# Cosine router after a state-space scan: work moved between VectorE, ScalarE and GpSimd, first steps reordered, three shared PSUM banks for the experts' turned tiles

## The chip, the cores and the metric

The program runs on one core of one Trainium2 chip. The metric is the device time in microseconds of one execution. Five engines run their own queues in order and meet at semaphores: TensorE (PE; its weight loads are listed apart as PEld), VectorE (DVE), ScalarE (ACT), GpSimd (POOL) and SyncE (SP, which here only issues DMAs).

## The reference

A Mamba-2 scan over 4 batches, 8 heads and 768 positions (head width 32, state width 16) gives 3072 tokens of 256 numbers. Each token then goes to one of 8 experts, the one whose embedding has the largest cosine with it, and its two-layer result is scaled by the softmax of that choice.

```python
for c in range(nc):                       # chunks of the sequence, state carried on
    cum = np.cumsum(la, axis=-1)          # la = log(clip(a))
    L = np.exp(cum[..., :, None] - cum[..., None, :]) * causal
    y_intra = np.einsum('bhij,bhjd->bhid', np.einsum('bhin,bhjn->bhij', Cc, Bc) * L, xc)
    y_inter = np.einsum('bhin,bhnd->bhid', Cc, state) * np.exp(cum)[..., None]
...
logits = xn @ en.T / tau                  # xn, en: rows over their norm + 1e-6
expert_idx = np.argmax(logits, axis=1)
h = np.maximum(x[mask] @ w1[e], 0.0)      # for every expert e
out[mask] = gate_w[mask, None] * (h @ w2[e])
```

## The kernel before

The scan cuts the sequence into 6 chunks of 128 positions. Decays are made as running products (`decays`) and put on the operands: C times the decay up to its position (`scale_c`, tile `cp`) and x times the inverse (`scale_x`, tile `xs`), so that the product C B^T needs only a causal mask. B is written twice with half of its state rows set to zero (`split_b`, tile `bz`). A pair p is two of a chunk's four batches, so there are 12 pairs, two for each chunk.

The order is written out by hand. `begin_scan` holds the first steps; `mamba` then runs steps s = 1 to 11. In step s TensorE makes the scores of pair s (`scores`, L467, into `pgA` and `pgB`), the outputs of pair s-1 (L499, L508, into `py`), in odd steps the sums for the next state (L526, into `pz`), the tokens of pair s-2 (`tokens`, L557, which also gives their logits), and the routing's matmuls: ranks (L353) in even steps, a table (L411) in odd ones. `masks` (L473 to 486) clears the acausal half of the scores: `pgA` by a multiplication on VectorE (L478), `pgB` by a copy on ScalarE (L477) and a selection in place on GpSimd (L484). ScalarE then copies the outputs (`yT`, L518) and the tokens (`yt`, L567). VectorE makes the next state from `pz` in odd steps (`states`: V at L542, T at L547, V only after ScalarE's `yt`), then the one-hot choice of expert (`pick`, L329 to L338, called the routing here; the ranks need it). In even steps it makes the places (`places`, L369 to L401, called the placing), and ScalarE a part of them (`hv`, L404). In ScalarE's queue `hv` stands ahead of the next step's mask copy.

SyncE loads a chunk's inputs two chunks ahead and the first expert's weights in parts, and stores the tokens' rows. GpSimd gathers rows for the experts by indirect DMA (`gather`, L708), takes a square root in `squares` (L723), and scatters the results (L796).

The experts (`moe`) run as jobs: two short ones for tokens known early and left over from them (256 and 160 rows), then eight of up to 416 rows in four blocks. A job turns its rows (`turn_x`, L750, two halves, each copied by VectorE at L752), goes up (8 blocks of L760, three PSUM banks in a ring), down (L775), and out (`out`, L789, four blocks turned back, scaled by ScalarE or VectorE, scattered). A ring hands out its banks in turn; a bank is written again only when its last reader is done. `turn_x` has a ring of one bank (3), `out` of two (6 and 7). `gates` makes the softmax factor; its exponential (L737) stands in ScalarE's queue among the `hT` copies.

Of the kernel before, what the change touches and what calls it, by code (L numbers as in the profile page):

```python
# [296 lines left out]

def norm_embeddings(k):
    nc = k.nc
    tau = k.en_tau  # L300
# [4 lines left out]
    nc.gpsimd.tensor_scalar(out=r[:], in0=r[:], scalar1=1e-6, scalar2=None, op0=ALU.add)
    nc.gpsimd.tensor_tensor(out=r[:], in0=r[:], in1=tau[:], op=ALU.mult)
    k.emb_r = r
    k.turn = k.mc.tile([128, 2, Y1], F32, name="turn")
    nc.gpsimd.tensor_copy(out=k.turn[:, 0, 0:128], in_=k.ident[:])
    blocks = lambda v: v.rearrange("p (a s d) -> p a s d", a=2, s=2)  # L310
    for i in range(2):
        nc.gpsimd.tensor_copy(out=blocks(k.turn[:, 1, E:])[:, :, i, :], in_=blocks(k.ident[:])[:, :, 1 - i, :])
# [160 lines left out]
def masks(k, p):  # L473
    nc = k.nc
    s = k.un[p] = Net()
    s.g = k.work.tile([128, 4, 4, Q], F32, name="g", tag="g")
    k.nc.scalar.copy(out=s.g[:, 2:4].rearrange("p q a i -> p q (a i)"), in_=k.pgB[:])  # L477
    nc.vector.tensor_tensor(  # L478
        out=s.g[:, 0:2].rearrange("p q a i -> p (q a) i"),
        in0=k.pgA[:].rearrange("p q (a i) -> p (q a) i", a=4),  # L480
        in1=bc(k.mask[:], [128, 8, Q], 1), op=ALU.mult,
    )
    g = s.g[:, 2:4].rearrange("p q a i -> p (q a) i")
    nc.gpsimd.affine_select(  # L484
        out=g, in_=g, pattern=[[0, 8], [1, Q]], compare_op=ALU.is_ge, fill=0.0, base=0, channel_multiplier=-1
    )
# [609 lines left out]
```

## Time and profile before

| what | time |
|---|---|
| three runs | 305.37, 308.0, 308.25 us; median 308.0 |
| profiled execution | 307.75 us; its span, from the first to the last instruction, 305.9 us |
| busy share of the span | PE 88%, DVE 37%, ACT 28%, POOL 38% |
| mean granted TensorE clock | 0.953 of full speed |
| scan and routing | from 0 to about 84 us |
| experts | from about 84 us to the end |

A row of the timeline shows what an engine did and, in brackets, how long it had stood before and what ended that. A row may merge several instructions; "x32" is their count. [...] Of a busy time of several engines in one stretch, only the engine whose waits are shortest sets the time there.

### The profile page before, as it was taken

How to read it: one execution, taken by the hardware profiler on the slowest of the kernel's cores; microseconds unless marked ns; L12 is line 12 of the kernel's file. 1: busy time of each engine (PE TensorE's matmuls, PEld its weight loads, DVE VectorE, ACT ScalarE, POOL GpSimd, SP SyncE). 2: the span in 40 equal slices, each digit the busy share in tenths (PEclk: the TensorE clock that was granted, in tenths of full speed). 3: DMA queues.
4: the chain of work that ended last, by engine and by line, in shares of the span. 5: the costliest groups of instructions: out<-in, count | busy, mean ns of one | idle time of the engine just before them, and what ended most of it. 6: DMA issues, size and time to landing. Idle time of an engine off the chain costs nothing.

```text
span 305.9 us, 5554 instructions
## 1 busy us (share of the span) xinstructions
PE 267.7 (88%) x2183; PEld 175.7 (57%) x2183; DVE 114.5 (37%) x352; ACT 84.2 (28%) x214; POOL 117.4 (38%) x142
## 2 busy tenths in 40 slices
PE   7388895897989699998999999999999999999980
PEld 6276784785868586554555555555555555555540
DVE  7048778369462342312321330422323042133110
ACT  2136574373323213121203212120330221122010
POOL 3955745464402626206503710740460172015004
PEclk9758999797899999999999999999999999999996
DMA  6801567263497155124340712424060020001001
GB/s 195 333 3 44 200 219 272 75 206 111 110 350 259 48 174 186 42 117 132 109 137 1 224 47 108 141 99 137 20 224 2 0 74 30 0 0 56 0 0 61
DMA packets 20781, 34.78 MB, mean 114 GB/s; under 512 B 2328, under 2 KB 13796, under 8 KB 20752
## 3 DMA queue, kind: packets, MB, share of 16 engines
q1 hardware_dynamic: 17712, 27.94, 27.2%
q0 software_dynamic: 2816, 6.40, 6.9%
q8 instruction: 18, 0.29, 0.4%
q14 instruction: 11, 0.09, 0.1%
q10 hardware_dynamic: 224, 0.06, 0.1%
HBM read 28.26 MB, written 6.65 MB: 114 GB/s over the span
## 4 chain that ended last, share of the span: by engine, by line
PE 50%; issue 26%; DVE 10%; POOL 7%; ACT 3%; DMA 2%; SPq 1%; POOLq 1%; DVEq 0%; ACTq 0%
PE bank L760 17%; PE bank L775 15%; POOL out_dram L796 3%; PE pz L557 3%; PE py L508 3%; PE pgA L467 3%; POOL xg L708 2%; PE py L499 2%; DVE g L478 2%; PE bank L789 2%; DMA in_t<-in_B_dram 1%; PE bank L750 1%; DVE T L547 1%; DVE xT L752 1%; DMA in_c<-in_CT_dram 1%
## 5 line engine op out<-in xcount | busy, mean ns | idle before, releaser
L760 PE MATMUL bank<-xT,w 128*128 128x416 f32 (+2 forms) x288 | 93.9, 477 | 2.0 <-ACT hT L764 1.9
L775 PE MATMUL bank<-hT,w 128*128 128x416 f32 (+2 forms) x288 | 91.7, 476 | 0.0
L760 PEld LDWEIGHTS bank<-xT,w 128*128 128x128 f32 x288 | 52.2, 190 | 36.6 <-issue 32.6
L775 PEld LDWEIGHTS bank<-hT,w 128*128 128x128 f32 x288 | 52.6, 190 | 34.8 <-issue 33.7
L723 POOL TENSOR_TENSOR gr<-gr,half 128x4 f32<-128x4 f32 (+1 forms) x9 | 8.7, 971 | 92.5 <-ACT sq L719 89.1
L796 POOL DMA_INDIRECT out_dram<-yo,to x30 | 29.2, 974 | 36.0 <-ACT yo L795 28.0
L766 DVE TENSOR_SCALAR hT<-bank 128x416 f32<-128x416 f32 (+2 forms) x33 | 18.2, 553 | 60.2 <-PE bank L760 55.8
L708 POOL DMA_INDIRECT xg<-rows,table x30 | 30.5, 1018 | 21.2 <-DVE to_u L440 13.1
L764 ACT ACTIVATE hT<-bank 128x416 f32<-128x416 f32 (+2 forms) x39 | 18.1, 469 | 62.1 <-PE bank L760 56.3
L467 PE MATMUL pgA<-cp,bz 32*128 32x128 f32 x192 | 17.3, 326 | 9.2 <-POOL bz L179 4.3
L734 DVE TENSOR_SCALAR gr<-gr 128x4 f32<-128x4 f32 (+1 forms) x9 | 1.5, 170 | 60.9 <-POOL gr L723 58.2
L484 POOL TENSOR_SCALAR_AFFINE_SELECT g<-g 128x1024 f32<-128x1024 f32 x12 | 13.4, 1114 | 27.4 <-ACT g L477 27.4
L779 ACT COPY yoT<-bank 128x416 f32<-128x416 f32 (+2 forms) x9 | 4.2, 467 | 66.4 <-PE bank L775 66.4
L467 PEld LDWEIGHTS pgA<-cp,bz 32*128 32x128 f32 x192 | 14.8, 227 | 10.5 <-POOL bz L179 4.5
L478 DVE TENSOR_TENSOR g<-pgA,mask 128x1024 f32<-128x1024 f32 x12 | 14.6, 1217 | 10.8 <-PE pgB L467 7.0
L467 PE MATMUL pgB<-cp,bz 32*128 32x128 f32 x192 | 17.4, 328 | 0.0
L750 PE MATMUL bank<-ident,xg 128*128 128x128 f32 x64 | 11.5, 273 | 6.6 <-DVE xT L752 6.6
L508 PE MATMUL py<-g,xs 128*32 128x128 f32 x384 | 15.2, 301 | 2.1 <-issue 2.1
L557 PE MATMUL pz<-turn,yT 128*128 128x136 f32 x96 | 15.9, 312 | 0.1
L477 ACT COPY g<-pgB 128x1024 f32<-128x1024 f32 x12 | 12.1, 1007 | 12.0 <-PE pgB L467 11.3
L750 PEld LDWEIGHTS bank<-ident,xg 128*128 128x128 f32 x64 | 7.8, 139 | 12.7 <-DVE xT L752 7.7
L467 PEld LDWEIGHTS pgB<-cp,bz 32*128 32x128 f32 x192 | 14.6, 225 | 0.0
(195 smaller groups left out, 272.8 us busy)
## 6 DMA issues: line engine op xcount, KB each, us to landing
w<-in_moe_w_dram SPq DMA_DIRECT2D x14, 1024.0 KB, 4.9
rows<-yt SPq DMA_DIRECT2D x12, 264.0 KB, 5.5
in_x<-in_x_dram SPq DMA_DIRECT2D x6, 512.0 KB
w<-in_moe_w_dram SPq DMA_DIRECT2D x8, 256.0 KB, 3.7
in_b<-in_BT_dram SPq DMA_DIRECT2D x6, 256.0 KB, 3.2
in_c<-in_CT_dram SPq DMA_DIRECT2D x6, 256.0 KB
in_t<-in_B_dram SPq DMA_DIRECT2D x6, 256.0 KB
xg<-rows,table POOLq DMA_INDIRECT x30
```

Of the source, the lines that this page charges most:

```text
L467: k.nc.tensor.matmul((k.pgA, k.pgB)[q // 2][:, q % 2, a : a + 128], lhsT=t.bz[r, v, b + i, :], rhs=t.cp[r, b + i, :], start=True, stop=Tru ...
L478: nc.vector.tensor_tensor(out=s.g[:, 0:2].rearrange("p q a i -> p (q a) i"), in0=k.pgA[:].rearrange("p q (a i) -> p (q a) i", a=4), in1=bc ...
L484: nc.gpsimd.affine_select(out=g, in_=g, pattern=[[0, 8], [1, Q]], compare_op=ALU.is_ge, fill=0.0, base=0, channel_multiplier=-1)
L508: nc.tensor.matmul(k.py[g : g + 32, v, 128 * i : 128 * i + 128], lhsT=t.xs[:, b + i, 4 * v + q, :], rhs=s.g[:, q, 2 * i + v, :], start=(c ...
L557: k.nc.tensor.matmul(k.pz[i][:, at : at + Y1], lhsT=yT[:, j, i, :], rhs=k.turn[:, j, :], start=(j == 0), stop=(j == 1), skip_group_check=True,
L708: s.k.nc.gpsimd.indirect_dma_start(out=s.x[0:p, i, 0:TOK], out_offset=None, in_=rows, in_offset=bass.IndirectOffsetOnAxis(ap=s.at[0:p, i : ...
L750: nc.tensor.transpose(t[:, o : o + p], s.x[0:p, i, Y1 * j : Y1 * j + 128], k.ident[:p, :p])
L760: nc.tensor.matmul(t, lhsT=s.w1[:, j, 128 * f : 128 * f + 128], rhs=s.xT[:, j, :], start=(j == 0), stop=(j == KD - 1))
L764: nc.scalar.activation(s.hT[:, f, :], t, ACT.Relu)
L766: nc.vector.tensor_scalar_max(s.hT[:, f, :], t, 0.0)
L775: nc.tensor.matmul(t, lhsT=s.w2[:, f, 128 * j : 128 * j + 128], rhs=s.hT[:, f, :], start=(f == 0), stop=(f == KF - 1))
L796: d = nc.gpsimd.indirect_dma_start(out=k.out[:, :], out_offset=bass.IndirectOffsetOnAxis(ap=s.to[0:p, i : i + 1], axis=0), in_=y[:p], in_o ...
```

## The change

- `split_b` runs on VectorE (for the first two chunks one half stays on ScalarE); before, GpSimd had a half of chunk 0 and both of chunk 1, ScalarE the rest.
- `scale_x` runs on VectorE, one pair in each step (before on GpSimd, two pairs in odd steps). `scale_c` runs on VectorE throughout (before on GpSimd from step 3 on), and stands ahead of `split_b`.
- `masks`: from step 3 on ScalarE copies both `pgB` and `pgA`, and GpSimd selects in both. In steps 0 to 2 `pgA` stays with VectorE.
- First steps: the small copies for `turn` come first on GpSimd and half of the routing's constants later; the embedding's norm is made later, part of it on VectorE; two of the fill matmuls that keep TensorE busy go. `inverse(k, 1)` moves from step 2 to 3, its turn from step 4 to 6.
- Experts: `turn_x` and `out` share one ring of banks 3, 6 and 7. The gathers of the first full job (`begin(1)`) are issued ahead of the first two jobs' squares, and both squares stand together.

```diff
-def split_b(k, c, halves=(0, 1), pool=()):
+def split_b(k, c, act=()):
     t = k.ld[c]
...
+    t.bz = k.work.tile([128, 2, NB, Q], F32, name="bz", tag="bz")
+    for v in range(2):
+        if v in act:
+            k.nc.scalar.activation(t.bz[:, v], t.bt[:], ACT.Copy, scale=k.tmask[:, v : v + 1])
+        else:
+            k.nc.vector.tensor_scalar(
                 out=t.bz[:, v], in0=t.bt[:], scalar1=k.tmask[:, v : v + 1], scalar2=None, op0=ALU.mult
             )
...
-def masks(k, p):
+def masks(k, p, both=True):
...
+    for h in range(2):
+        ps = (k.pgB, k.pgA)[h][:].rearrange("p q (a i) -> p (q a) i", a=4)
+        g = s.g[:, 2 - 2 * h : 4 - 2 * h].rearrange("p q a i -> p (q a) i")
+        if h == 1 and not both:
+            nc.vector.tensor_tensor(out=g, in0=ps, in1=bc(k.mask[:], [128, 8, Q], 1), op=ALU.mult)
+            continue
+        nc.scalar.copy(out=g, in_=ps)
+        nc.gpsimd.affine_select(
+            out=g, in_=g, pattern=[[0, 8], [1, Q]], compare_op=ALU.is_ge, fill=0.0, base=0, channel_multiplier=-1
+        )
...
-    decays(k, 0)
-    norm_embeddings(k)
-    place_consts(k)
-    split_b(k, 0, pool=(1,))
+    first, later, consts = decays(k, 0), decays(k, 1), place_consts(k)
+    turn_consts(k)
+    next(consts)
+    next(first)
+    next(first)
+    split_b(k, 0, act=(0,))
     spread_decays(k, range(4))
     inverse(k, 0)
...
-    fill(k, 2, k.pgA[:, 0, 0:Q])
+    fill(k, 1, k.pgA[:, 0, 0:Q])
     keep_decays(k, 1)
     scores(k, 0)
-    decays(k, 1)
-    scale_x(k, 0, nc.gpsimd)
-    scale_x(k, 1, nc.gpsimd)
-    masks(k, 0)
+    next(later)
+    next(later)
+    norm_embeddings(k)
+    masks(k, 0, both=False)
     scale_c(k, 1, spread_at(k, 0))
+    scale_x(k, 0, nc.vector)
...
-    split_b(k, 1, pool=(0, 1))
+    split_b(k, 1, act=(0,))
...
+    scale_x(k, 1, nc.vector)
+    next(consts)
...
-            masks(k, s)
+            masks(k, s, both=s > 2)
...
-        if s == 4:
+        if s == 6:
             turn_inverse(k, 1, k.py[:, 0, 256:384])
...
+        if s % 2 and c < NC - 1:
+            states(k, c)
+        if s + 2 < NP:
+            scale_c(k, s + 2)
         if s % 2 == 0 and s // 2 + 1 < NC:
             split_b(k, s // 2 + 1)
-        if s % 2 and c < NC - 1:
-            states(k, c)
...
-        if s + 2 < NP:
-            scale_c(k, s + 2, eng=nc.vector if s < 3 else nc.gpsimd)
-        if s % 2 and c + 1 < NC:
-            scale_x(k, 2 * c + 2, nc.gpsimd)
-            scale_x(k, 2 * c + 3, nc.gpsimd)
+        if s + 1 < NP:
+            scale_x(k, s + 1, nc.vector)
...
-        if s == 2:
+        if s == 3:
             inverse(k, 1)
...
-    k.bank = {"hp": ring(banks[0:3]), "xt": ring(banks[3:4]), "yp": ring(banks[4:6]), "ot": ring(banks[6:8])}
+    turned = ring([banks[3], banks[6], banks[7]])
+    k.bank = {"hp": ring(banks[0:3]), "xt": turned, "yp": ring(banks[4:6]), "ot": turned}
...
     load_all_weights(k, 2)
+    begin(1)
     j0.down(0)
     j0.squares()
-    begin(1)
+    jobs[1].squares()
     j0.gates()
     j0.down(1)
     jobs[1].turn_x()
-    jobs[1].squares()
     jobs[1].gates()
```

The first place is VectorE's queue in step 5, from `states` to the start of the routing (L329 before, L332 of the change): before, and then of the change.

```order
L542 TENSOR_TENSOR V<-T,pz_91 128x2x64
L542 TENSOR_TENSOR V<-T,pz_92 128x2x64
L547 TENSOR_TENSOR T<-V,whole 128x256
L420 TENSOR_TENSOR acc<-acc,pz_91 128x64
L329 TENSOR_REDUCE m<-yt 128x4
```

```order
L546 TENSOR_TENSOR V<-T,pz_91 128x2x64
L546 TENSOR_TENSOR V<-T,pz_92 128x2x64
L551 TENSOR_TENSOR T<-V,whole 128x256
L270 TENSOR_TENSOR cp<-in_c,fr 128x256
L423 TENSOR_TENSOR acc<-acc,pz_91 128x64
L279 TENSOR_TENSOR xs<-in_x,rT 128x512
L332 TENSOR_REDUCE m<-yt 128x4
```

A `cp` and an `xs` now stand between the state and the routing.

The second place is VectorE's queue further on, from the routing's last instruction (L338 before, L341 of the change) to the second of the placing: before, and then of the change.

```order
L338 TENSOR_REDUCE ob<-ob 128x8
L478 TENSOR_TENSOR g<-pgA,mask 128x1024
L369 TENSOR_TENSOR oh<-pz_92,ob 128x32
L385 TENSOR_REDUCE row<-oh 128x4
L387 TENSOR_SCALAR hl<-row 128x4
```

```order
L341 TENSOR_REDUCE ob<-ob 128x8
L270 TENSOR_TENSOR cp<-in_c,fr 128x256
L182 TENSOR_SCALAR bz<-in_b,tmask 128x512 x2
L279 TENSOR_TENSOR xs<-in_x,rT 128x512
L372 TENSOR_TENSOR oh<-pz_92,ob 128x32
L388 TENSOR_REDUCE row<-oh 128x4
```

The mask of step 6 is gone from between routing and placing; a `cp`, two halves of `bz` and an `xs` stand there.

The third place is TensorE's queue where one full job's rows are turned, ahead of its `down` (bank names carry their number): before, and then of the change.

```order
L750 MATMUL bank3_1398<-ident_129,xg0_219 128x128 x3
L750 MATMUL bank3_1398<-ident_129,xg0_219 128x32
L750 MATMUL bank3_1398<-ident_129,xg0_219 128x128 x3
L750 MATMUL bank3_1398<-ident_129,xg0_219 128x32
L775 MATMUL bank4_1399<-hT_1677,w2_1_68 128x416 x8
```

```order
L758 MATMUL bank6_1407<-ident_129,xg0_319 128x128 x3
L758 MATMUL bank6_1407<-ident_129,xg0_319 128x32
L758 MATMUL bank7_1408<-ident_129,xg0_319 128x128 x3
L758 MATMUL bank7_1408<-ident_129,xg0_319 128x32
L783 MATMUL bank4_1405<-hT_1683,w2_1_68 128x416 x8
```

The two halves now lie in two banks; the order of the instructions is the same.

## Rows read from the trace of the kernel before

**Rows 1.** Busy time by stretch (the view of windows): start and end, length in us, busy us and instructions of TensorE (PE), its weight loads (PEld), VectorE (DVE), ScalarE (ACT) and GpSimd (POOL), then the granted TensorE clock as a share of full speed, the DMA share and GB/s. The stretches are steps 5 and 6, ten microseconds that hold step 9, and the end of the scan.

```profile
38.80:49.80 11.00, 8.82 (x253) 7.49 (x253) 8.97 (x22) 7.17 (x14) 6.66 (x7) 1.00 0.67 227
60.00:70.00 10.00, 10.00 (x287) 8.77 (x280) 7.56 (x19) 7.06 (x14) 6.90 (x8) 1.00 0.68 214
72.90:84.10 11.20, 10.89 (x194) 8.99 (x195) 6.69 (x28) 3.94 (x8) 3.40 (x3) 0.71 0.46 122
```

**Rows 2.** The timeline of all engines in the first steps: start and length in us, engine, line, operation, out<-in, and in brackets the idle time before it and what ended it.

```profile
4.97 0.95 DVE L220 RECIPROCAL r<-f 128x128 f32<-128x128 f32 x1
...
11.48 1.58 POOL L179 TENSOR_SCALAR bz<-in_b,tmask 128x512 f32<-128x512 f32 x1
...
13.11 0.58 PE L467 MATMUL pgA<-cp,bz 32*128 32x128 f32 x2 [4.35 <-POOL bz L179]
...
14.35 0.42 PE L467 MATMUL pgB<-cp,bz 32*128 32x128 f32 x2
...
16.68 1.22 PE L192 MATMUL py<-zero 128*128 128x128 f32 x4 [1.91 <-ACT fr L606]
```

**Rows 3.** The timeline of TensorE alone at the scores of step 3, same columns.

```profile
29.44 0.38 PE L467 MATMUL pgA<-cp,bz 32*128 32x128 f32 x2 [1.43 <-DVE g L478]
...
30.55 0.67 PE L499 MATMUL py<-cp,T 32*32 32x128 f32 x32
```

**Rows 4.** The timeline of VectorE alone: the first instruction of `states` (V) in steps 3, 5, 7 and 9, and what follows V of step 7 in VectorE's queue: the routing of that step, a mask (L478), and the first and the last instructions of the placing in step 8.

```profile
33.78 0.29 DVE L542 TENSOR_TENSOR V<-T,pz 128x128 f32<-128x128 f32 x1 [1.83 <-ACT yt L567]
...
43.70 0.57 DVE L542 TENSOR_TENSOR V<-T,pz 128x128 f32<-128x128 f32 x2 [1.20 <-ACT yt L567]
...
58.03 0.57 DVE L542 TENSOR_TENSOR V<-T,pz 128x128 f32<-128x128 f32 x2 [5.23 <-ACT yt L567]
58.63 0.42 DVE L547 TENSOR_TENSOR T<-V,whole 128x256 f32<-128x256 f32 x1
...
59.10 0.18 DVE L329 TENSOR_REDUCE m<-yt 128x4 f32<-128x32 f32 x1
...
60.36 1.21 DVE L478 TENSOR_TENSOR g<-pgA,mask 128x1024 f32<-128x1024 f32 x1
...
62.57 0.19 DVE L369 TENSOR_TENSOR oh<-pz,ob 128x32 f32<-128x32 f32 x1 [1.00 <-ACT yt L567]
...
63.52 0.69 DVE L392 TENSOR_TENSOR low<-lows,hf 128x512 bf16<-128x512 f32 x1
64.13 0.28 DVE L397 TENSOR_TENSOR hi<-his,hf 128x128 f32<-128x128 f32 x1
...
67.02 0.57 DVE L542 TENSOR_TENSOR V<-T,pz 128x128 f32<-128x128 f32 x2 [1.14 <-ACT yt L567]
```

**Rows 5.** The timeline of ScalarE alone: the end of step 8 with step 9, and the last placing inside the scan.

```profile
64.45 0.40 ACT L404 ACTIVATE hv<-hi,part 128x128 bf16<-128x128 f32 x1 [0.69 <-DVE hi L397]
64.76 0.99 ACT L477 COPY g<-pgB 128x1024 f32<-128x1024 f32 x1
65.65 0.59 ACT L518 COPY yT<-py 128x512 f32<-128x512 f32 x1
66.60 0.66 ACT L567 COPY yt<-pz 128x264 f32<-128x264 f32 x2 [0.36 <-PE pz L411]
...
74.74 0.40 ACT L404 ACTIVATE hv<-hi,part 128x128 bf16<-128x128 f32 x1 [2.50 <-DVE hi L397]
```

**Rows 6.** The timelines of GpSimd alone and of VectorE alone: a selection and a VectorE operation that overlap, the same VectorE operation without overlap, and two that give a price by size.

```profile
3.38 0.23 DVE L203 TENSOR_SCALAR aw<-a 128x126 f32<-128x126 f32 x1 [0.59 <-DMA emb<-in_moe_expert_emb_dram]
...
29.31 0.41 DVE L267 TENSOR_TENSOR cp<-in_c,fr 128x256 f32<-128x256 f32 x1
...
46.39 1.09 POOL L484 TENSOR_SCALAR_AFFINE_SELECT g<-g 128x1024 f32<-128x1024 f32 x1
...
46.51 1.00 DVE L332 TENSOR_TENSOR oh<-oh,order 128x32 f32<-128x32 f32 x1
...
59.54 0.19 DVE L332 TENSOR_TENSOR oh<-oh,order 128x32 f32<-128x32 f32 x1
```

**Rows 7.** What TensorE waited for (the view of waits), the first two lines from 14 to 130 us, the last two from 130 to 306 us: engine, line and releaser, us in total, times, the longest.

```profile
PE bank L750 <- DVE xT L752: 3.2, 4, 1.3
PE py L508 <- issue: 2.1, 1, 2.1
...
PE bank L750 <- DVE xT L752: 3.4, 5, 0.7
PE bank L789 <- ACT yo L795: 2.1, 6, 0.4
```

**Rows 8.** The timeline of TensorE alone: the second half of one expert's turned tiles, and the third and fourth blocks of one job's way out.

```profile
182.52 0.72 PE L750 MATMUL bank<-ident,xg 128*128 128x128 f32 x4 [0.68 <-DVE xT L752]
...
198.19 0.69 PE L789 MATMUL bank<-ident,yoT 128*128 128x128 f32 x4 [0.34 <-ACT yo L795]
```

**Rows 9.** The timelines of GpSimd alone and of TensorE alone around the gates of the first two jobs.

```profile
99.15 0.74 POOL L723 TENSOR_TENSOR gr<-gr,half 128x2 f32<-128x2 f32 x1 [3.42 <-issue]
105.01 0.74 POOL L723 TENSOR_TENSOR gr<-gr,half 128x2 f32<-128x2 f32 x1
...
102.39 1.57 PE L760 MATMUL bank<-xT,w 128*128 128x160 f32 x8
...
106.86 3.08 PE L760 MATMUL bank<-xT,w 128*128 128x160 f32 x20 [1.92 <-ACT hT L764]
```

More of the change, by code (lines that the diff above doesn't have):

```diff
@@ L80, in early_consts @@
     )
-    ones = m.tile([128, 128], F32, name="ones")
+    ones = k.ones = m.tile([128, 128], F32, name="ones")
     g.memset(ones[:], 1.0)
@@ L111, in place_consts @@
     k.his = ramp("his", E * NT, pattern=[[32, E], [1, NT]])
+    yield
     k.order = ramp("order", E, pattern=[[-1, E]], base=E)
@@ L120, in place_consts @@
     k.xg = [c.tile([128, NT, 2 * Y1], F32, name=f"xg{i}") for i in range(3)]
+    yield
 def mask_columns(k):
@@ L208, in decays @@
     v.tensor_tensor_scan(out=f, data0=aw, data1=k.heads[p], initial=0.0, op0=ALU.mult, op1=ALU.add)
+    yield
     w = k.mc.tile([128, 2], F32, name=f"w{kk}")
@@ L215, in decays @@
         v.memset(k.f[0:32, 0, HQ : HQ + 1], 1.0)
+    yield
 def inverse(k, kk):
@@ L295, in embeddings, with turn_consts @@
     k.en_tau = tau
+def turn_consts(k):
+    k.turn = k.mc.tile([128, 2, Y1], F32, name="turn")
+    k.nc.gpsimd.tensor_copy(out=k.turn[:, 0, 0:128], in_=k.ident[:])
+    blocks = lambda v: v.rearrange("p (a s d) -> p a s d", a=2, s=2)
+    for i in range(2):
+        k.nc.gpsimd.tensor_copy(out=blocks(k.turn[:, 1, E:])[:, :, i, :], in_=blocks(k.ident[:])[:, :, 1 - i, :])
 def norm_embeddings(k):
     nc = k.nc
-    tau = k.en_tau
     sq = k.mc.tile([E, DM], F32, name="emb_sq")
-    r = k.mc.tile([E, 1], F32, name="emb_r")
+    r = k.emb_r = k.mc.tile([E, 1], F32, name="emb_r")
     nc.scalar.activation(sq[:], k.en[:], ACT.Square, accum_out=r[:])
     nc.gpsimd.tensor_tensor(out=r[:], in0=r[:], in1=k.half[0:E, 0:1], op=ALU.pow)
[L305 to L312, printed above, removed]
 def turn_embeddings(k, ps):
-    nc = k.nc
-    nc.vector.reciprocal(out=k.emb_r[:], in_=k.emb_r[:])
-    nc.vector.tensor_scalar_mul(k.en[:], k.en[:], k.emb_r[:])
+    nc, r = k.nc, k.emb_r
+    nc.vector.tensor_scalar(out=r[:], in0=r[:], scalar1=1e-6, scalar2=k.en_tau[:], op0=ALU.add, op1=ALU.mult)
+    nc.vector.reciprocal(out=r[:], in_=r[:])
+    nc.vector.tensor_scalar_mul(k.en[:], k.en[:], r[:])
     for j in range(2):
@@ L476, in masks @@
     s.g = k.work.tile([128, 4, 4, Q], F32, name="g", tag="g")
[L477 to L486, printed above, removed]
+    for h in range(2):
[8 more added lines that the diff above has]
+        )
 def outputs(k, p):
@@ L608, in begin_scan @@
     )
-    fill(k, 2, k.py[:, 1, 0:Q])
+    fill(k, 1, k.py[:, 1, 0:Q])
     spread_decays(k, (4, 5))
@@ L612, in begin_scan @@
     keep_decays(k, 5)
-    split_b(k, 1, pool=(0, 1))
+    split_b(k, 1, act=(0,))
     scores(k, 1)
     between(k, 0, 1)
-    masks(k, 1)
+    masks(k, 1, both=False)
     scale_c(k, 2)
+    scale_x(k, 1, nc.vector)
+    next(consts)
     keep_decays(k, 2)
```

7 lines of the change are left out of this document (removed).

## Prediction

> **What bounds the kernel now.** I read the view of windows first, to see which engine has no time left in which stretch. [...] Then I read the timeline of the first steps, where TensorE stands for 4.35 us in the middle of the first scores, because GpSimd makes the second half of `bz` only at 11.48, behind its small constants [rows 2]. Third, the view of waits: in the experts, which are TensorE from end to end, the only regular waits are for one PSUM bank (L750 for the copy of the turned tile, L789 for the scaled output) [rows 7, 8]. So time can come from three places: the start, the serial chain between two V's, and the bank waits.
>
> **The first steps.** `f` is ready at 4.95, when the reciprocal starts [rows 2]. GpSimd's small copies now run beside VectorE's decays; I allow 0.4 us for that. VectorE then makes half of `bz`. No row shows this operation on VectorE: from below the 0.23 us of 126 elements, from above the 0.69 us of a 512-element operation with two inputs [rows 4, 6]. I take 0.44, between them, and 0.36 to the next start (VectorE starts an operation about 0.08 before the one ahead ends, as L392 and L397 show). [...] With the reciprocal (0.95), its memset and `cp` (0.41) [rows 2, 6] the scores of step 0 start at 7.4 and, at 1.1 to 1.2 us for a pair's scores [rows 3], end at 8.6. Before they ended at 14.77: **6.2 us earlier**. The next steps keep their order on the path (mask, `cp`, a copy on ScalarE, fill 1.9 us after the scores, as at 16.68). What is new there is that `xs` stands behind the mask on VectorE, so that the sums of step 1 wait for it, about 1 us; one fill less and a shorter backlog in step 2 give about as much back. The V of step 3 should come at 27.4 instead of 33.78, a lead of 6.4 us.
>
> **The chain from V to V.** In the old and the new order one chain closes over two steps: V, then the routing on VectorE, the placing, `hv` on ScalarE, behind `hv` in ScalarE's queue the mask copies, `yT` and `yt`, and V again, which waits for `yt`. Start to start, from [rows 4, 5, 6]: V 0.60; T and `acc` 0.47 (58.63 to 59.10); routing 1.26 (59.10 to 60.36); placing up to `hv` 1.88 (62.57 to 64.45); `hv` 0.31; first copy 0.89; `yT` 0.59; `yt` to V 0.42 (66.60 to 67.02). The change takes VectorE's mask (1.21) out and puts in, all ahead of the placing: two `cp` at 0.33, two `xs` at 0.61 (as L392, the nearest with 512 elements and two inputs in SBUF), two `bz` at 0.36; and on ScalarE a second mask copy, 0.89, of the same shape as the first. Sum: 0.60 + 0.47 + 1.26 + 1.88 + 0.31 + 0.89 + 0.59 + 0.42 + 0.66 + 1.22 + 0.72 + 0.89 = **9.9 us**. [...]
>
> Then the holding. While GpSimd's selection ran from 46.39 to 47.48, a 32-element VectorE operation took 1.00 us instead of 0.19 and ended with it [rows 6]. Two selections follow the even step's scores. Those scores begin when the second copy frees `pgA`, 1.0 us before V (0.59 + 0.42); so the selections run from 1.1 to 3.3 us after V, exactly beside `cp`, `xs` and the routing. From below the holding costs nothing, from above all four selections of two steps, 4.4 us. I take 2.0, nearly the two that meet VectorE's work; the odd step's two end beside `yT`, `yt` and V, which has an input in PSUM. That makes **11.9 us** for two steps. [...]
>
> From 27.4 the V's come at 40.3 (step 3 also has the reciprocal that was in step 2, 1.0 us), 52.2 and 64.1, against 43.70, 58.03 and 67.02. The 2.1 us in which TensorE waited for nothing visible in step 7 [rows 7] falls into time that TensorE would idle anyway. From the last V to `hv` it was 7.7 us (74.74); now 0.60 + 0.47 + 0.33 + 0.61 + 1.26 + 0.61 + 1.88 + 0.2 for the shift + 2.0 held = 8.0, so `hv` comes at 72.1. **The scan ends 2.6 us earlier**: most of the lead of 6.4 is given back to the longer chain. The routing ends 5.3 us after V, TensorE is there about 3 us after V (half a pair, 4 us and a little, from the start of those scores, 1.0 before V): it should stand for 2 us at L356 in each pair of steps. `scale_x` and `scale_c` leave GpSimd at no price but this, since GpSimd has no other queue behind them than the selections.
>
> **The experts.** With three banks the second half of the turned tiles no longer waits for the copy of the first: 0.68 us [rows 8], seven times, 4.76. (Its cover: the copies have the whole of `down`, 11 us, before `up` needs them.) On the way out the third block finds a free bank; the fourth waits for the first one's scaling, which ends just then: of 0.34, 0.29 is gained, six times (2.1 us in all [rows 7]), 1.74. For the first job, half of the longest wait (1.3) returns, 0.55; the copy of its first half is itself late behind the placing. The gathers of the first full expert, moved past two square roots on GpSimd's queue, take the 5.1 us between 99.89 and 105.01 [rows 9]; the first root therefore runs 1.7 us later, and VectorE, waiting for it, copies the next job's tiles late, so that its `up` starts at 103.7 instead of 102.39. But both roots are then done, and the wait of 1.92 us for ScalarE (106.86), which stood behind the second gate's exponential, is gone: TensorE gets there at 106.2, 0.7 earlier, bank wait included. Sum: **7.75 us**.
>
> **Sum.** The profiled execution took 307.75 us (span 305.9; the median of the three runs is 308.0). 307.75 - 2.6 - 7.75 = 297.4; I say **297.5 us**.
>
> **The rivals.** (A) As above, 294 to 300.5: chance 0.52. (B) Nothing is held. For it: in [rows 4] the pair from step 7 to 9 shows no holding, since the selections fell elsewhere. Against: the selections now follow V by a fixed order. Pairs of 9.9 and a last stretch of 6.0 bring `hv` to 64.2 (27.4 + 10.9 + 9.9 + 9.9 + 6.0 = 64.1), 10.6 earlier: 289.4. Chance 0.15. (C) The holding is half as long again with TensorE partly at the lower clock, pairs of 13.1 and a last stretch of 9.2: `hv` at 76.9, 2.2 later than before: 302.2. For it: after a wait TensorE has been slow (clock 0.71 at the end of the scan [rows 1]). Chance 0.20. [...] Chance 0.05. (E) The banks bring nothing, because TensorE then waits in `down` for `hT` instead: 297.5 + 6.5 = 304. Against: `hT`'s last tile is copied ahead of the turned tiles. Chance 0.08.
>
> **The numbers.** The three runs of before lie 0.9% apart, so 1% is about what a measurement can tell. Faster by over 1% (under 304.9): A, B, most of C and half of E, 0.87. Slower (over 311.1): most of D, 0.04. The same: the rest, 0.09. The range from 290 to 304 leaves out D, half of E and the far end of B, under 2 in 10; the bounds of the holding (0 and 4.4 us a pair) reach from 289 to about 307, and I keep only the part that carries the chance.
>
> **What would show it.** Right: no wait of TensorE above 1 us inside the first scores, and their end near 8.6; V's near 27, 40, 52 and 64; L356 waiting some 2 us for the routing, each time beside long `cp`, `xs` or `oh` operations on VectorE; no wait at L758, next to none at L797; each expert about 1 us shorter. Wrong: V's less than 10.5 us apart (no holding, B), a granted clock near half of full through the steps 5 to 10 (D), or a wait that appears in `down`.

## The result, and the profile after

The changed kernel takes 295.25 us (median of 4 runs, 293.78 to 297.13) beside 308.12 us before on the same chip: a ratio of 0.961, 95% interval 0.952 to 0.971. The forecast was 297.5, range 290 to 304. The profiled execution took 293.78 us, of which the span is 292.0 (before 305.9).

First the start. The timeline of all engines, with start and length in us, engine, line, operation, and in brackets the idle time before it and its cause:

```profile
5.00 0.48 DVE L182 TENSOR_SCALAR bz<-in_b,tmask 128x512 f32<-128x512 f32 x1
...
8.05 0.39 PE L470 MATMUL pgB<-cp,bz 32*128 32x128 f32 x4
...
9.57 1.09 POOL L488 TENSOR_SCALAR_AFFINE_SELECT g<-g 128x1024 f32<-128x1024 f32 x1 [0.81 <-ACT g L487]
9.83 1.37 DVE L279 TENSOR_TENSOR xs<-in_x,rT 128x512 f32<-128x512 f32 x1
10.17 0.49 PE L193 MATMUL py<-zero 128*128 128x128 f32 x2 [1.73 <-ACT fr L613]
```

The half of `bz` that was made at 11.48 [rows 2] is made at 5.00, and the scores of step 0 end at 8.44 (8.05 and 0.39). The 4.35 us of [rows 2] are gone; the fill comes at 10.17 in place of 16.68. `xs` starts during a selection and takes 1.37; started ahead of one it takes 0.69 (below).

Next VectorE's timeline from the V of step 7 to that of step 9, which answers to [rows 4]:

```profile
49.76 0.57 DVE L546 TENSOR_TENSOR V<-T,pz 128x128 f32<-128x128 f32 x2 [2.72 <-ACT yt L571]
...
50.71 0.42 DVE L270 TENSOR_TENSOR cp<-in_c,fr 128x256 f32<-128x256 f32 x1
...
51.17 0.69 DVE L279 TENSOR_TENSOR xs<-in_x,rT 128x512 f32<-128x512 f32 x1
51.77 0.18 DVE L332 TENSOR_REDUCE m<-yt 128x4 f32<-128x32 f32 x1
51.99 0.86 DVE L334 TENSOR_TENSOR oh<-yt,m 128x32 f32<-128x32 f32 x1
52.89 1.01 DVE L335 TENSOR_TENSOR oh<-oh,order 128x32 f32<-128x32 f32 x1
53.93 0.18 DVE L336 TENSOR_REDUCE m<-oh 128x4 f32<-128x32 f32 x1
...
61.10 0.57 DVE L546 TENSOR_TENSOR V<-T,pz 128x128 f32<-128x128 f32 x2 [2.72 <-ACT yt L571]
```

GpSimd's two selections of the step before (step 7) and of that stretch (step 8), in its own timeline:

```profile
48.12 2.13 POOL L488 TENSOR_SCALAR_AFFINE_SELECT g<-g 128x1024 f32<-128x1024 f32 x2 [4.67 <-ACT g L487]
51.39 2.46 POOL L488 TENSOR_SCALAR_AFFINE_SELECT g<-g 128x1024 f32<-128x1024 f32 x2 [1.14 <-ACT g L487]
```

Two operations of 32 elements take 0.86 and 1.01 us (0.19 alone [rows 6]): they lie inside the selections, 51.39 to 53.85. `cp` had ended by then (51.13), and `xs` had begun (51.17) and is not longer than usual; here it is the selections that are longer, 2.46 where the two of step 7 take 2.13. V to V is 11.34. The shortest two steps before, from step 7 to 9, took 9.0 us (58.03 to 67.02 [rows 4]), and in the ten microseconds that hold step 9 TensorE was busy for 10.00 us at a granted clock of 1.00 [rows 1]; 9.0 is taken from this, as an estimate, for what two steps cost TensorE itself. V to V is now 2.3 longer, and TensorE waits.

What TensorE waited for, from 0 to 130 us and then from 130 us on (engine, line, releaser, total, times, longest):

```profile
PE pz L356 <- DVE ob L338: 4.1, 3, 1.5
PE pgA L470 <- ACT g L487: 4.0, 3, 1.4
...
PE bank L758 <- ACT yt L571: 1.1, 1, 1.1
```

```profile
PE bank L797 <- DVE yoT L789: 1.9, 2, 1.3
PE bank L797 <- ACT yo L803: 0.2, 1, 0.2
```

The routing (L356) is waited for three times, as forecast. A second wait, of the scores for ScalarE's second copy, is new. In the experts the 3.4 us of [rows 7] are gone, and the 2.1 us are 0.2; the 1.9 us for `yoT` stood before too.

The turned tiles and the way out of one expert, and the next one's tiles, on TensorE:

```profile
171.50 1.32 PE L758 MATMUL bank<-ident,xg 128*128 128x128 f32 x8
...
186.82 1.34 PE L797 MATMUL bank<-ident,yoT 128*128 128x128 f32 x8
196.38 1.32 PE L758 MATMUL bank<-ident,xg 128*128 128x128 f32 x8
```

All eight matmuls run without a gap, where [rows 8] show 0.68 and 0.34. An expert takes 24.88 us (171.50 to 196.38); before, the same two places were 25.92 apart.

### The profile page after: what moved, and what is told of

Read it like the earlier page. It is cut to its first block, busy times and chain, and to the rows that moved or that the text cites. A ratio compares the mean times of both kernels' runs of the same rounds, so it can differ in the third digit from the quotient of the medians.

```text
span 292.0 us, 5541 instructions
## 1 busy us (share of the span) xinstructions
PE 261.9 (90%) x2179; PEld 171.3 (59%) x2179; DVE 118.0 (40%) x373; ACT 87.3 (30%) x216; POOL 105.8 (36%) x127
## 4 chain that ended last, share of the span: by engine, by line
PE 41%; issue 26%; DVE 13%; POOL 7%; DMA 5%; ACT 4%; SPq 1%; POOLq 1%; ACTq 0%; DVEq 0%
PE bank L768 17%; PE bank L783 16%; POOL out_dram L804 4%; DMA in_x<-in_x_dram 3%; POOL xg L716 3%; DVE xs L279 2%; ACT g L487 2%; PE bank L758 2%; DMA xg<-rows,table 1%; PE py L512 1%; DVE oh L335 1%; PE pz L561 1%; DVE low L395 1%; DVE cp L270 1%; DVE oh L334 1%
## 5 line engine op out<-in xcount | busy, mean ns | idle before, releaser
L488 POOL TENSOR_SCALAR_AFFINE_SELECT g<-g 128x1024 f32<-128x1024 f32 x21 | 23.7, 1151 | 35.5 <-ACT g L487 35.5
L470 PE MATMUL pgA<-cp,bz 32*128 32x128 f32 x192 | 15.5, 305 | 5.6 <-ACT g L487 4.0
L470 PEld LDWEIGHTS pgA<-cp,bz 32*128 32x128 f32 x192 | 13.1, 207 | 6.6 <-ACT g L487 4.3
L470 PE MATMUL pgB<-cp,bz 32*128 32x128 f32 x192 | 15.5, 305 | 0.0
L561 PE MATMUL pz<-turn,yT 128*128 128x136 f32 x96 | 14.9, 297 | 0.1
L561 PEld LDWEIGHTS pz<-turn,yT 128*128 128x128 f32 x96 | 12.3, 194 | 2.1 <-issue 1.0
L470 PEld LDWEIGHTS pgB<-cp,bz 32*128 32x128 f32 x192 | 13.0, 205 | 0.0
L727 ACT ACTIVATE sq<-xg 128x256 f32<-128x256 f32 x32 | 12.9, 408 | 0.0
L512 PEld LDWEIGHTS py<-g,xs 128*32 128x32 f32 x384 | 11.0, 119 | 3.1 <-issue 2.8
```

Of the source, the lines that this page charges most:

```text
L470: k.nc.tensor.matmul((k.pgA, k.pgB)[q // 2][:, q % 2, a : a + 128], lhsT=t.bz[r, v, b + i, :], rhs=t.cp[r, b + i, :], start=True, stop=Tru ...
L488: nc.gpsimd.affine_select(out=g, in_=g, pattern=[[0, 8], [1, Q]], compare_op=ALU.is_ge, fill=0.0, base=0, channel_multiplier=-1)
L512: nc.tensor.matmul(k.py[g : g + 32, v, 128 * i : 128 * i + 128], lhsT=t.xs[:, b + i, 4 * v + q, :], rhs=s.g[:, q, 2 * i + v, :], start=(c ...
L561: k.nc.tensor.matmul(k.pz[i][:, at : at + Y1], lhsT=yT[:, j, i, :], rhs=k.turn[:, j, :], start=(j == 0), stop=(j == 1), skip_group_check=True,
L727: nc.scalar.activation(sq[:], s.x[:, i].rearrange("p (j w) -> p j w", j=2)[:, :, 0:128], ACT.Square, accum_out=s.r[:, i : i + 1],)
```

## The experiments

Twelve kernels ran. "V 3" is the start of V in step 3; "pairs" are the distances to the V's of steps 5, 7 and 9; "xT" is the copy of the first job's first turned tile; all from VectorE's timeline of the profiled execution, in us. Ratios are to the kernel before on the same chip; the medians come from several chips, so a difference of medians between two rows is rougher than the ratios.

| kernel | V 3 | pairs | xT | span | median | ratio, 95% |
|---|---|---|---|---|---|---|
| before | 33.78 | 9.92 14.33 8.99 | 85.38 | 305.9 | 308.12 | |
| changed | 26.63 | 11.78 11.35 11.34 | 79.71 | 292.0 | 295.25 | 0.952 to 0.971 |
| banks_only | 34.07 | 9.93 14.79 9.04 | 85.35 | 298.9 | 300.99 | 0.969 to 0.986 |
| gates_only | 34.22 | 9.93 13.05 9.48 | 85.22 | 307.9 | 307.42 | 0.992 to 1.002 |
| bz_only | 28.59 | 9.93 14.92 9.48 | 81.47 | 303.7 | 303.06 | 0.977 to 0.991 |
| three_parts | 28.81 | 9.93 13.33 9.78 | 79.53 | 291.8 | 294.07 | 0.952 to 0.963 |
| scaled_on_gpsimd | 27.29 | 11.45 11.79 12.34 | 81.10 | 295.1 | 297.03 | 0.957 to 0.972 |
| no_selections | 27.92 | 11.03 9.93 9.85 | 75.24 | 289.5 | 291.34 | 0.939 to 0.954 |
| hv_on_vector | 25.62 | 11.75 11.27 11.26 | 79.99 | 293.3 | 295.48 | 0.956 to 0.968 |
| pick_first | 25.39 | 12.75 11.85 11.25 | 80.06 | 293.7 | 295.63 | 0.953 to 0.969 |
| half_masks | 24.79 | 11.26 10.75 10.74 | 76.50 | 290.5 | 292.24 | 0.945 to 0.960 |
| even_select | 26.95 | 10.85 10.43 10.43 | 77.84 | 291.8 | 292.94 | 0.945 to 0.960 |
| late_pick | 27.08 | 11.19 10.07 10.07 | 75.74 | 288.0 | 290.14 | 0.936 to 0.948 |
| late_pick_bank | 26.21 | 11.18 10.08 10.07 | 75.18 | 288.6 | 290.49 | 0.931 to 0.946 |

### Parts of the change alone

**banks_only**, the kernel before with the one ring.

```diff
-    k.bank = {"hp": ring(banks[0:3]), "xt": ring(banks[3:4]), "yp": ring(banks[4:6]), "ot": ring(banks[6:8])}
+    turned = ring([banks[3], banks[6], banks[7]])
+    k.bank = {"hp": ring(banks[0:3]), "xt": turned, "yp": ring(banks[4:6]), "ot": turned}
```

> The kernel before, with the experts' turned tiles sharing three banks and nothing else of the change. By the forecast: first-half waits of the turned tiles gone, 7 x 0.68 = 4.76 us, out 6 x 0.29 = 1.74, first job 0 to 0.55: 6.5 to 7.0 us less, about 301 us, no wait at the turn of a full expert. Rival (the wait only moves into the down or up matmuls): within 1 us of before, with a new wait there of about 0.7 per expert.

Measured: 6.75 us less. From xT to the end of the span it is 213.55 us (298.9 - 85.35) against 220.5 before: 6.95. No new wait stands in the experts. Rival E of the prediction is refuted.

**gates_only**, the kernel before with the six lines around `begin(1)` in the new order.

> The kernel before, with only the order of the late gates changed (gathers of the first full expert ahead of both square roots, both square roots ahead of both gates). By the forecast 0.5 us less (the wait of 1.92 us of TensorE near 107 is gone, its up starts about 1.3 later). If the wait was real slack of TensorE and the gathers delay nothing, up to 1.9 less. Rival (the gathers on GpSimd's queue now delay the first root, and all behind it): 0 to 1.5 us more.

Measured: 0.3 us less, interval from 0.8% less to 0.2% more: alone it can't be told from nothing. Its profiled execution (309.7 us) doesn't show the gain either: the eight matmuls with which the second job's `up` starts took 2.30 us there (from 104.98), where the kernel before has 1.57 [rows 9] at a granted clock of 1.00 from 100 to 110 us.

**bz_only**, the kernel before with one operation moved.

```diff
-    split_b(k, 0, pool=(1,))
+    t = k.ld[0]
+    t.bz = k.work.tile([128, 2, NB, Q], F32, name="bz", tag="bz")
+    nc.scalar.activation(t.bz[:, 0], t.bt[:], ACT.Copy, scale=k.tmask[:, 0:1])
+    nc.vector.tensor_scalar(out=t.bz[:, 1], in0=t.bt[:], scalar1=k.tmask[:, 1:2], scalar2=None, op0=ALU.mult)
```

> The kernel before, with the second half of the first bz made on VectorE (one operation of 512 elements behind the decays) in place of GpSimd, and nothing else of the change. By the forecast the scores of step 0 end near 8.6 to 9 instead of 14.77 and the V of step 3 comes near 28 instead of 33.78; the old steps behind it keep their spacing of 9.9, 14.3 and 9.0, so hv comes 5 to 6 us earlier and the time is about 302. Rival (the later steps of the start wait for GpSimd's scaled x and constants, so that the lead is lost at once): V of step 3 no more than 2 us earlier, time within 2 us of before.

Measured: 5.2 us less; V 3 is 5.2 earlier, and the first pair behind it is that of before; the next two are 1.1 longer together, and xT is 3.9 earlier in this execution (305.51 us, the slowest of its four). One operation on another engine is most of the gain of the start.

**three_parts**, the three edits above in one kernel; the scan's order is that of before.

> The kernel before with three parts of the change: the first bz's second half on VectorE, the shared banks and the order of the late gates; the scan's steps are those of before, with scaled x and C and half the masks where they were. If the parts add, 308.2 - 5.2 - 6.8 - 0.6 = 295.6. Theory (moving the scaled x and C to VectorE gained about what the selections of all masks on GpSimd cost): within 1.5 us of the changed kernel (295.25), hv and the first job's tile at 81.5 as with bz alone against 79.7. Rival (the new order of the scan is itself worth 2 us or more): 297 to 300. Rival the other way (the new order costs): 291 to 293.5.

Measured: 294.07 against 295.25, with intervals that overlap. So the theory holds: the rest of the change (scaled C and x on VectorE, all masks selected on GpSimd, the new order of the first steps) is worth nothing that can be told. The traces show two parts that about cancel: in the changed kernel V 3 comes 2.2 earlier, its three pairs are 1.4 longer together (34.47 and 33.04), and V to `hv` is 0.5 longer (7.62 and 7.09). Against banks_only the stretch behind xT is 212.27 (291.8 - 79.53), 1.3 less. That is the gates: from the second job's turned tiles to the third's TensorE takes 8.76 us in banks_only and 7.48 here, both at a granted clock of 1.00.

**scaled_on_gpsimd**, the changed kernel.

```diff
-            scale_c(k, s + 2)
+            scale_c(k, s + 2, eng=nc.vector if s < 3 else nc.gpsimd)
...
-            scale_x(k, s + 1, nc.vector)
+            scale_x(k, s + 1, nc.vector if s < 3 else nc.gpsimd)
```

> The changed kernel, with the scaled C and x of step 3 and later back on GpSimd, behind the selections in its queue. GpSimd has 4 x 1.11 + 2 x 1.10 + 2 x 0.73 = 8.1 us of work in two steps, VectorE 1.88 less. Theory (GpSimd's work holds VectorE, and the scaled tiles come late behind the selections): V to V 11.5 to 13.5, total 0 to 6 us more than the changed kernel, with sums or scores waiting for GpSimd. Rival (VectorE's length alone counts): V to V 9.5 to 10.5, total 3 to 5 less.

Measured: 1.8 us more by the medians, with intervals that overlap; the pairs of 11.8 and 12.3 show that VectorE's length does not count alone. GpSimd's scaled C and x, with the memset behind them, hold it as selections do. VectorE's two `bz` take 0.87 together in the changed kernel (first view) and 2.88 here (second view), beside GpSimd's `cp`, `xs` and a memset (54.97 to 57.82):

```profile
54.85 0.87 DVE L182 TENSOR_SCALAR bz<-in_b,tmask 128x512 f32<-128x512 f32 x2
```

```profile
55.22 2.88 DVE L182 TENSOR_SCALAR bz<-in_b,tmask 128x512 f32<-128x512 f32 x2
```

### The chain from V to V

**no_selections** leaves out GpSimd's selections from step 3 on, so the scores of those steps keep their upper triangles.

```diff
+        if both:
+            continue
         nc.gpsimd.affine_select(
```

> The changed kernel without GpSimd's selections from step 3 on: the scores of those steps keep their upper triangles, so this leaves out part of the masks. Theory holding (the selections cost the chain 1.5 us per two steps through the held routing on VectorE): V to V falls from 11.35 to about 9.85, the last V comes 4.5 earlier and hv 5 to 6 earlier, total 5 to 6 us less than the changed kernel. Rival (held VectorE work would have waited for its inputs anyway, or the chain has slack): V to V stays above 11.0, total within 1 us.

Measured: pairs of 9.93 and 9.85, where the prediction summed 9.9 for the chain that is not held. The two operations of the routing take 0.19 again:

```profile
41.18 0.19 DVE L334 TENSOR_TENSOR oh<-yt,m 128x32 f32<-128x32 f32 x1
41.40 0.19 DVE L335 TENSOR_TENSOR oh<-oh,order 128x32 f32<-128x32 f32 x1
```

So holding is 11.35 - 9.89 = 1.46 us a pair. From V to `hv` it is 6.84 here (48.88 to 55.72) and 8.33 in the changed kernel (49.76 to 58.09); from `hv` to the next V it is 3.01 in both. xT is 4.5 earlier, the time only 3.9, the span 2.5: in the 25 us behind xT the granted clock was 0.93 here and 1.00 in the changed kernel. V 3 is 1.3 later than there: with no selections in its queue GpSimd makes its memsets for the experts already in step 2, and VectorE stands beside them (its timeline, then GpSimd's):

```profile
19.61 3.90 DVE L258 TENSOR_SCALAR whole<-g_raw,tmask 128x16 f32<-128x16 f32 x2
20.73 2.78 DVE L485 TENSOR_TENSOR g<-pgA,mask 128x1024 f32<-128x1024 f32 x1
```

```profile
20.57 2.89 POOL L688 MEMSET xg<- 128x1088 f32 x3
```

The two `whole` take 1.19 in the changed kernel.

**hv_on_vector** takes ScalarE out of the circle.

```diff
-    nc.scalar.activation(k.hv[:, :, 1], hi[:], ACT.Copy, scale=k.part[:])
+    nc.vector.tensor_scalar(out=k.hv[:, :, 1], in0=hi[:], scalar1=k.part[:], scalar2=None, op0=ALU.mult)
```

> The changed kernel, with the second half of hv (the one of 128 elements that ScalarE scales) made on VectorE, so that ScalarE's mask copies no longer stand behind the routing in ScalarE's queue. Theory chain (V, routing, placing, hv on ScalarE, two mask copies, yT, yt, V sets the pace): the circle is broken, VectorE's own work for two steps is 8.6 us with 1.5 held, so V to V falls from 11.35 towards TensorE's 9.0, I say 10.0 to 10.4; three pairs and the last stretch give 3 to 5 us, about 291. Rival TensorE (it is its own waits for the second mask copy and the routing that set the pace, whatever stands in ScalarE's queue): V to V stays at 11.2 to 11.4, time within 1 us of the changed kernel.

Measured: pairs of 11.27; no gain, as the rival said. Yet its reason is not the one. In the timeline of all engines:

```profile
44.58 2.61 POOL L488 TENSOR_SCALAR_AFFINE_SELECT g<-g 128x1024 f32<-128x1024 f32 x2 [2.17 <-ACT g L487]
...
44.78 1.46 DVE L395 TENSOR_TENSOR low<-lows,hf 128x512 bf16<-128x512 f32 x1
...
46.17 1.17 DVE L400 TENSOR_TENSOR hi<-his,hf 128x128 f32<-128x128 f32 x1
...
48.23 0.66 ACT L571 COPY yt<-pz 128x264 f32<-128x264 f32 x2 [2.31 <-PE pz L414]
```

ScalarE's copies did come sooner, and so did the odd step's selections, which now hold the placing: `low` and `hi` take 2.63 in place of 0.97. And a second circle shows: `yt` waits for the table (L414), which TensorE runs after the tokens into the same tile `pz` and which waits for `hv`. The held placing lies in that circle; how long it would be without the 1.66 us of holding wasn't measured.

**pick_first** puts `pick` ahead of `scale_c` and `scale_x` in the odd steps.

> The changed kernel, with the routing (the part from the maximum to ob) put ahead of the scaled C and the scaled x in VectorE's queue in the odd steps. The routing then lies ahead of the two selections, and scaled C and x beside them. Theory 1 (only operations that start during a selection are held, and scaled C and x are held there like the routing was): V to V falls by 0.5 to 0.8 to about 10.7, and TensorE's wait for the routing goes; total 1.5 to 2.5 us less than the changed kernel. Theory 2 (scaled C and x are never held, being longer; only the small operations are): V to V 9.85, total 4 to 5 us less. Rival (place in the queue is of no matter, the selections cost the same wherever they fall): V to V 11.3, no change.

Measured: the pairs are no shorter, so neither theory's number came, and the rival's did; what is held follows theory 1. (TensorE's granted clock was 0.95 from 24 to 60 us; in the changed kernel it was 1.00 from 20 to 60.) VectorE's timeline:

```profile
51.15 0.19 DVE L334 TENSOR_TENSOR oh<-yt,m 128x32 f32<-128x32 f32 x1
51.37 0.19 DVE L335 TENSOR_TENSOR oh<-oh,order 128x32 f32<-128x32 f32 x1
...
52.19 1.05 DVE L270 TENSOR_TENSOR cp<-in_c,fr 128x256 f32<-128x256 f32 x1
...
53.30 1.44 DVE L279 TENSOR_TENSOR xs<-in_x,rT 128x512 f32<-128x512 f32 x1
```

The routing is free, and `cp` and `xs` are held instead, 1.05 for 0.42 and 1.44 for 0.69, 1.38 together where the routing lost 1.5. The selections run from 51.84 to 54.19: `cp`, started in the first, ends 0.27 after it (53.24), and `xs`, started in the second, ends 0.54 after it (54.73); beside the 0.42 and 0.69 that they take alone, my estimate is that each does most of its work only then. `acc`, behind `cp`, comes late for the tokens as well (TensorE waits 4.4 us for it in 3 times).

**half_masks** and **even_select** change one argument of `masks`: pgA's half on VectorE in all steps, or in the odd steps alone.

```diff
-            masks(k, s, both=s > 2)
+            masks(k, s, both=False)
```

```diff
-            masks(k, s, both=s > 2)
+            masks(k, s, both=s > 2 and s % 2 == 0)
```

> The changed kernel, with half of the masks (pgA's) on VectorE in all steps, as before the change, so that GpSimd selects 12 times and not 21 and ScalarE copies pgB's half alone. The chain of 9.85 loses one copy of 0.89 on ScalarE and takes one or two multiplications of 1.2 on VectorE; the holding falls from 1.5 to 0.5 or nothing. Theory (chain with the holding): V to V 10.2 to 11.4, that is nearly as long as 11.35, total within 2.5 us of the changed kernel and rather under it. Rival (moving the masks off VectorE was the gain of the scan): V to V 12.5 to 13.5, total 4 to 6 us more.

> The changed kernel, with pgA's masks of the odd steps on VectorE again, those of the even steps on GpSimd as changed. In the chain one copy of 0.89 on ScalarE goes, and VectorE's multiplication lies beside ScalarE's copy and yT; the holding of the routing by two selections stays 1.5. Theory chain: V to V 11.35 - 0.89 = 10.45, about 0.3 under the kernel with half of the masks (10.74), time 291 to 293. Rival (VectorE's multiplication delays V): V to V 11.3 to 11.7.

Measured: pairs of 10.74 and of 10.43 (10.45 was worked out), medians 3.0 and 2.3 us under the changed kernel, with intervals that overlap with its own; the evidence is the pairs, every one of which is shorter. In even_select `hv` to V is 2.10 (56.56 to 58.66) where the changed kernel takes 3.01, and V to `hv` is 8.33 in both: ScalarE's second copy, which the selection of pgA on GpSimd needs, costs 0.91 a pair. That all masks are selected on GpSimd is the part of the change that costs.

**late_pick** is half_masks with the routing behind the even step's multiplication in VectorE's queue.

```diff
             masks(k, s, both=False)
+            if s % 2 == 0 and s >= 4:
+                pick(k, (s - 4) // 2)
...
-        if s % 2 and s >= 3:
+        if s == NP - 1:
             pick(k, (s - 3) // 2)
```

> Half of the masks on VectorE in all steps, and the routing put behind that multiplication of the even step in VectorE's queue. The multiplication reads PSUM, which no run has shown held, and it covers the one selection that the routing met (0.67 lost at one operation). Theory: no long operation in the routing, V to V 10.74 - 0.67 = 10.05, last V and hv 2 to 2.7 us earlier than with half of the masks alone, time 289 to 291. Rival (TensorE then waits for ob and gives it back, or the multiplication is held too): V to V 10.6 to 10.9, time 292 to 293.

Measured: pairs of 10.07, where 10.05 was worked out. The timeline of all engines:

```profile
50.13 1.26 POOL L488 TENSOR_SCALAR_AFFINE_SELECT g<-g 128x1024 f32<-128x1024 f32 x1 [1.42 <-ACT g L487]
...
50.36 1.22 DVE L485 TENSOR_TENSOR g<-pgA,mask 128x1024 f32<-128x1024 f32 x1
...
51.70 0.19 DVE L334 TENSOR_TENSOR oh<-yt,m 128x32 f32<-128x32 f32 x1
```

The multiplication reads PSUM, starts inside the selection and takes its usual 1.22; the routing behind it starts after the selection's end (51.39) and is not held. The interval of this kernel, 0.936 to 0.948, lies under that of the changed kernel; it overlaps with that of half_masks, whose median is 2.1 us higher.

**late_pick_bank** gives the first job's turned tiles banks 3 and 4.

```diff
+    k.bank["xt"] = ring([banks[3], banks[4]])
     j0.turn_x()
+    k.bank["xt"] = turned
```

> The kernel late_pick, with the first job's two turned tiles in banks 3 and 4 (4 held y in the scan) in place of 3 and 6 (6 holds pz, and yt is copied out of it late). Theory: the wait of 1.06 to 1.4 us of TensorE between the two halves goes; its up starts 0.3 to 0.5 earlier, since the copy of the first half waits behind the placing on VectorE. Rival (the copies set the start anyway): no difference, or under 0.3.

Measured: the wait between the halves is gone, and TensorE waits for the copy instead:

```profile
75.65 1.99 PE L770 MATMUL bank<-xT,w 128*128 128x256 f32 x8 [1.12 <-DVE xT L762]
```

This `up` starts 18.11 us after the last V, in late_pick 18.12. The rival holds: the copy, behind the placing on VectorE, sets that start.

## Why the prediction was right, and where its sizes were off

The mechanism was right in the start, in the circle and in the experts; what VectorE loses to the selections was right in kind and wrong in which operations lose it. The forecast lay 2.25 us over the median. Against its own execution it was 3.5 us too long: the span fell by 13.9, not 10.35. Up to xT the gain is 5.67 us (85.38 - 79.71), behind it 8.2 (220.5 - 212.3). The term that was mis-sized is "The scan ends 2.6 us earlier": `hv` came at 68.72, 6.0 earlier. That is 3.4 us too little, in four pieces.

- **The start**, forecast 27.4 for V 3, measured 26.63: 0.77. The scores of step 0 ended at 8.44 (8.6); the terms named for their start add up to about 7.1 and not 7.4, and they started at 7.08. Five executions that share VectorE's instructions up to V 3 (the changed kernel, hv_on_vector, no_selections, pick_first, scaled_on_gpsimd) put it between 25.39 and 27.92, so this piece is not told from the spread, whose causes stand below.
- **The holding**, taken as 2.0 a pair, measured 1.46: about 1.6 over three pairs. The step that failed is "exactly beside `cp`, `xs` and the routing". The sum let the selections begin 1.1 us after V; they began 1.63 after it (51.39). By then `cp` was done and `xs` had started, and only the routing was held, 0.67 and 0.82; in the first steps, where `xs` starts inside a selection, it is held (1.37). Here the order of starts decided, and the changed kernel's trace shows it both ways: VectorE waits in one case (1.37 for 0.69), the two selections stretch to 2.46 from 2.13 in the other. The 2.0 was an estimate between 0 and 4.4 from one held operation (1.00 for 0.19 [rows 6]); it reckoned with what lies beside a selection and not with which of the two starts first.
- **The inverse**, taken as 1.0 in the first pair: that pair is 0.43 longer than the next (11.78 and 11.35), which leaves 0.6.
- **The last stretch**, V to `hv`, taken as 8.0, is 7.62 (61.10 to 68.72): 0.4. Between `hv` and xT 0.35 is lost again, which the sum had not. ScalarE's timeline:

```profile
68.72 0.40 ACT L407 ACTIVATE hv<-hi,part 128x128 bf16<-128x128 f32 x1 [2.13 <-DVE hi L400]
```

The circle itself was summed well, in its halves too: 9.9 without holding (6.8 to `hv`, 3.1 behind it), and 9.89 in no_selections (6.84 and 3.01). `bz` was a little short: alone it took 0.48 where 0.44 was taken, and two took 0.79 start to start where 0.72 was summed. But it is not one circle. hv_on_vector shows another, through the table and `yt`, as long with the held placing in it; and the orders of VectorE's queue that were run only choose which operations meet the selections, unless one that reads PSUM does (late_pick). TensorE's wait at L356 was 1.4 a time, not 2; its wait for pgA, 1.3 a time, was missed. That it costs nothing itself is argued, not shown: TensorE waits for the routing behind it in any case.

**The experts**: forecast 7.75, measured 8.2. The banks gave 6.95 where 7.05 was summed, and the gates 1.3 where 0.7 was. The 0.55 for the first job (half of 1.3 would be 0.65) was not there: bank 6 is late by `yt` (1.06 at L758), and without that wait the copy sets the start (late_pick_bank). An expert gained 1.04, not 0.97, which makes up for it.

**The rivals.** B (nothing held) gave 289.4; no_selections, which is B, measured 291.34. D, a granted clock near half of full in the steps 5 to 10, did not come: it was 1.00 from 20 to 60 us and 0.81 from 60 to 70. No run shows the 294 at the low end of A; with the routing alone held, 1.46 a pair, the time was 295.25. E fell with banks_only. C needed pairs of 13.1.

**What the parts are worth.** The start's operation 5.2 us, the banks 6.8, the gates 0.3 to 1.3: about 12.3 to 13.3 of the 12.9, by medians that are each known to some 2 us. The rest of the change, its largest part in the diff, is a gain and a loss that cancel as far as three_parts can tell.

**Why the same first steps differ by 2.5 us.** VectorE's timeline in the changed kernel and then in pick_first, which has the same instructions there, at the mask and the `xs` of step 1:

```profile
13.51 1.23 DVE L485 TENSOR_TENSOR g<-pgA,mask 128x1024 f32<-128x1024 f32 x1 [1.44 <-PE pgA L470]
...
14.99 1.58 DVE L279 TENSOR_TENSOR xs<-in_x,rT 128x512 f32<-128x512 f32 x1
```

```profile
12.76 1.22 DVE L485 TENSOR_TENSOR g<-pgA,mask 128x1024 f32<-128x1024 f32 x1 [0.69 <-PE pgA L470]
...
14.24 0.68 DVE L279 TENSOR_TENSOR xs<-in_x,rT 128x512 f32<-128x512 f32 x1
```

The views of windows from 12 to 16 us, in the same order (columns as in [rows 1]; the granted clock is the third number from the end):

```profile
12.00:16.00 4.00, 3.77 (x74) 2.88 (x70) 2.56 (x5) 3.93 (x7) 1.34 (x2) 0.62 0.88 337
```

```profile
12.00:16.00 4.00, 2.62 (x90) 1.87 (x82) 3.24 (x8) 3.92 (x7) 1.47 (x2) 1.00 0.96 366
```

In pick_first, at a granted clock of 1.00, the scores of step 1 take 1.27 us (11.44 to 12.71), in the changed kernel, at 0.62, 2.10 (11.37 to 13.47), so the mask starts 0.75 later. That puts the start of `xs` behind that of GpSimd's selection (14.65) instead of ahead of it (14.53 in pick_first), and being held adds 0.9; the operations behind it give 0.4 of that back. From VectorE's copy of the first state (17.90 and 16.66) to V 3 both take 8.73. In scaled_on_gpsimd the clock was 0.82 from 9 to 12 us and 0.71 from 12 to 16 (mask at 14.17, V 3 at 27.29), in hv_on_vector 1.00 and 0.57 (12.99 and 25.62); in no_selections GpSimd's memsets add 1.6. So the granted clock and, through it, the order of starts make most of the spread.

Left open: why the granted clock falls in one execution and not in another of the same instructions, there and in the stretch of the first job, where it was 0.93 in some executions and 1.00 in others (about 1.7 us: behind xT half_masks took 214.0, late_pick 212.3).

## What to carry to other kernels

Where VectorE and GpSimd share a chain, list for each GpSimd operation what VectorE starts in its time. Here `oh` and `xs`, each with two SBUF inputs, were held to the end of the selection in which they started, or longer (1.01 for 0.19, 1.37 for 0.69). `xs` started ahead of one took 0.69, and a mask that reads PSUM took 1.22 inside one: so start the first kind earlier, or put the second there. A chain that closes over two steps is well summed start to start from rows, but look for the second circle before breaking the first. And run the small edits of a large change alone: here three of them gave all of it that could be told.

## What the runs showed of the hardware

- What was held followed the order of starts: `xs` took 0.69 when it began 0.22 before a selection (51.17 and 51.39, the changed kernel) and 1.44 when it began inside one (pick_first); the two selections took 2.46 in place of 2.13 when VectorE began first.
- Operations with one SBUF input tile were held too: two `bz` took 2.88 in place of 0.87 beside GpSimd's multiplications and a memset (scaled_on_gpsimd). Two `whole` of 16 elements took 0.37 in half_masks, 1.19 beside a selection (19.84 to 20.93, the changed kernel) and 3.90 up to the end of GpSimd's memsets (23.51 and 23.46, no_selections). But `ob` (0.19 at 42.80) and `cp` (0.42 at 43.17), started inside a memset of the changed kernel (42.45 to 43.45), were not held. Nor were three that read PSUM and started inside a selection: the mask (1.22, late_pick), `acc` (0.21 at 53.16, pick_first) and V (0.57 at 49.76, the changed kernel). One mask behind the held `whole` took 2.78.
- With the early `bz` TensorE's granted clock was also low for a shorter time. The view of windows from 16 to 20 us (start and end, length, busy us and instructions of PE, PEld, DVE, ACT and POOL, granted clock, DMA share, GB/s), before and then after:

```profile
16.00:20.00 4.00, 3.32 (x30) 3.09 (x34) 1.61 (x6) 0.21 (x2) 4.00 (x3) 0.50 0.02 4
```

```profile
16.00:20.00 4.00, 3.13 (x86) 2.65 (x87) 3.21 (x11) 1.53 (x5) 1.36 (x9) 1.00 0.04 13
```

Behind the wait of 4.35 us the granted clock was 0.50 from 12 to 24 us. With the early `bz` alone (bz_only) it was 0.50 from 12 to 16 us, 0.69 from 16 to 20 and 1.00 from 20 to 24; in the changed kernel it was 0.50 from 12 to 15 us, and 1.00 from 16 to 60; in pick_first it was 1.00 all the way to 24 us.
